# Attention followed by soft-MoE slots on one core: first v cast by the DMA and the second pair's loads issued sooner, warming matmuls ahead of the MoE, last two expert matrices in column halves, output of two batches stored in halves

## The chip, the cores and the metric

The kernel runs on 1 core of one Trainium2 chip. The metric is the device time of one execution in microseconds (us), median of several runs. A profile gives one execution: its span, from the first to the last instruction, is about 1.8 us below the measured time. Engines: PE (matmul), PEld (weight load into PE), DVE, ACT, POOL (whose queue issues the casting DMAs), SP (whose queue issues the stores). To evacuate a tile is to copy it from PSUM, where PE writes, to SBUF. A warming matmul multiplies zeros and its result is thrown away; it is there to keep PE busy, in the hope of keeping its clock up. The granted clock is given as a share: 1.00 is full, 0.50 half. Names in the traces: sc scores, siT slot inputs, hp layer 1, sp layer 2, op output; tpq, tpk and tpv are transposes of q, k and v.

## The reference

```python
# q, k, v: [4 batches, 8 heads, 768, 64] f32; masks: full causal or sink + window, by head
a = softmax(mask(q @ k.T / 8)); x = (a @ v) as [3072 tokens, 512]
logits = x @ phi                              # 3072 x 32 slots
d = softmax(logits, over tokens); slot_input = d.T @ x
for e in range(8):                            # 4 slots each
    h = relu(slot_input[e] @ w1[e])           # 512 -> 1024
    slot_out[e] = h @ w2[e]                   # 1024 -> 512
c = softmax(logits, over slots)
return c @ slot_out                           # 3072 x 512 f32
```

Every output row needs every expert, and the first softmax runs over all tokens. So nothing can be stored before the last attention block and the last weight matrix are in. The inputs are 18.9 MB of q, k, v and 33.6 MB of weights, all f32; the output is 6.29 MB.

## The kernel before

Attention runs over 16 pairs of heads. Beside it the casting queue loads q, k, v of later pairs and the 16 weight matrices (f32 in DRAM, bf16 in SBUF). The parts that matter here:

```python
# start: pair 0 uncast by SP and ACT, cast on DVE and ACT; pairs 1 and 2 by the casting queue
at.load_first("q", nc.sync, stage[0]); at.load_first("k", nc.scalar, stage[1])
at.load_first("v", nc.sync, stage[2])
nc.scalar.dma_start(ri, ...)                  # retrieval flags, 8 KB
at.warm(20)                                   # matmuls on zeros
...
at.load(1); at.load(2)
...
at.transpose(0, "q"); at.transpose(0, "k"); at.warm(3); at.evac(0, "q")
nc.vector.tensor_single_scalar(rne, ri ...)   # waits for the flags
...
at.evac(0, "k"); cast("v", 2, slice(0, 512), nc.vector)
# ... attention ...
# last matrices: 13 whole ones are queued in order, the last in two row halves
# MoE: 4 layer-1 blocks, then layer 2 of 8 experts over two PSUM tiles of 256 columns
for e in range(2, NE): layer2(e)
nc.scalar.activation(slot_out[:, :256], sp[0], ACT.Copy, scale=rcol)
nc.vector.tensor_scalar_mul(slot_out[:, 256:], sp[1], rcol)
# output: matmul, scale on ACT or DVE, store whole rows, 1 to 3 rows of 2 KB per partition
for b in range(B):
    for m in ((1, 2, 3) if b == 0 else (3, 3)):
        ...
        nc.sync.dma_start(ov[:, r:r + m, :], ot[:, :m, :])
```

The softmax here doesn't subtract the row's maximum and nothing guards it: scores larger than these inputs give would overflow.

## Time and profile before

| | kernel before |
|---|---|
| time, median (lowest to highest) | 154.51 us (154.14 to 155.01) |
| span of the profiled run | 152.7 us |
| layer 1 of the MoE starts | 121.49 us |
| last weight bytes move | 132.2 us (only a trickle from 131) |
| first output bytes move | 135.75 us |
| output bytes | 6.29 MB in 15.35 us |

The prediction shows the other views that matter.

```profile
DMA packets 14423, 33.51 MB, mean 219 GB/s; under 512 B 1856, under 2 KB 10496, under 8 KB 12480
q1 hardware_dynamic: 2240, 7.14, 12.5%
```

The second line is SP's queue, the stores and a few first loads: 2240 packets for 7.14 MB, 3.2 KB on average. The casting queue's GB/s count bytes written; it reads twice as many.

### The profile page before, as it was taken

Reading aid. Unit: us, or ns where it says so; the run is one execution under the profiler, and the core shown is the slowest. Engines: PE = TensorE matmul, PEld = TensorE weight load, DVE = VectorE, ACT = ScalarE, POOL = GpSimd, SP = SyncE. Lnnn points to the kernel's source line nnn. Section 1 sums busy time; section 2 is a strip of 40 time slices with the busy share of each in tenths; the row PEclk is TensorE's granted clock in tenths of the full one; section 3 lists DMA queues with packets and bytes.
Section 4 is the critical chain, followed back from the end, with each engine's and each line's share of the span. In section 5 each row is a group of like instructions: output and inputs, shape, how many; then the busy total and the mean of one; then the engine's idle time right before and its main releaser. Section 6 shows DMA issues by size and latency. Waiting matters only on the chain.

```text
span 152.7 us, 5567 instructions
## 1 busy us (share of the span) xinstructions
PE 130.1 (85%) x2397; PEld 86.9 (57%) x2398; DVE 116.2 (76%) x284; ACT 112.5 (74%) x176; POOL 40.2 (26%) x75
## 2 busy tenths in 40 slices
PE   7679998999899999999999999999977799998000
PEld 4436666576577666767767576776636525853000
DVE  6279769989989799898979989888995315189400
ACT  3326779999899899899989889998995224289000
POOL 7624534316243340614425145400000000000000
PEclk9955579999999999999999999999999758999855
DMA  4999999999999999999999999999999999149995
GB/s 135 209 210 203 228 196 227 196 229 197 205 228 194 227 198 225 195 212 222 197 226 198 225 193 215 225 212 212 217 221 210 212 211 181 36 165 416 414 414 240
DMA packets 14423, 33.51 MB, mean 219 GB/s; under 512 B 1856, under 2 KB 10496, under 8 KB 12480
## 3 DMA queue, kind: packets, MB, share of 16 engines
q0 software_dynamic: 11808, 25.63, 88.2%
q1 hardware_dynamic: 2240, 7.14, 12.5%
q10 hardware_dynamic: 352, 0.40, 1.0%
q8 instruction: 18, 0.29, 0.7%
q14 instruction: 5, 0.04, 0.1%
HBM read 52.50 MB, written 6.29 MB: 385 GB/s over the span
## 4 chain that ended last, share of the span: by engine, by line
DVE 42%; PE 32%; ACT 11%; DMA 4%; issue 3%; DVEq 0%; ACTq 0%
DVE xb L162 9%; PE pv L149 7%; ACT pT L123 6%; DVE pT L136 6%; PE sc L114 6%; DVE ot L590 5%; DVE xT L176 5%; DVE pT L133 5%; DMA ri<-in_is_retrieval_dram 4%; DVE vb L103 4%; PE tpx L170 4%; PE hp L516 4%; PE tpv L78 3%; ACT pT L119 3%; PE sp L545 2%
## 5 line engine op out<-in xcount | busy, mean ns | idle before, releaser
L123 ACT ACTIVATE pT<-sc,fb 128x512 bf16<-128x512 f32 (+1 forms) x96 | 52.6, 620 | 4.3 <-PE sc L114 2.8
L119 ACT ACTIVATE pT<-sc 128x1024 bf16<-128x1024 f32 (+1 forms) x48 | 44.8, 952 | 7.3 <-PE sc L114 6.7
L149 PE MATMUL pv<-vb,pT 128*128 128x65 bf16 x672 | 38.0, 197 | 3.6 <-DVE pT L133 2.0
L114 PE MATMUL sc<-qT,kT 64*128 64x256 bf16 (+3 forms) x320 | 36.6, 292 | 0.9 <-DVE kT L91 0.9
L149 PEld LDWEIGHTS <-pT 128*128 128x128 bf16 x672 | 27.1, 99 | 15.4 <-issue 6.9
L136 DVE TENSOR_TENSOR pT<-pT,msk 128x1024 bf16<-128x1024 bf16 (+1 forms) x32 | 19.7, 615 | 0.0
L69 POOL DMA_DIRECT2D qr<-in_q_dram x15 | 9.8, 652 | 34.4 <-PE tpq L78 34.4
L162 DVE TENSOR_TENSOR xb<-pv,rs 128x384 bf16<-128x384 f32 x32 | 17.8, 557 | 1.1
L114 PEld LDWEIGHTS <-kT 64*128 64x128 bf16 x320 | 10.5, 95 | 8.9 <-issue 1.7
L69 POOL DMA_DIRECT2D vr<-in_v_dram x15 | 9.5, 632 | 11.4 <-PE tpv L78 10.7
L176 DVE COPY xT<-tpx 128x768 bf16<-128x768 bf16 (+1 forms) x17 | 9.1, 534 | 4.4 <-PE tpx L170 4.3
L69 POOL DMA_DIRECT2D kr<-in_k_dram x15 | 9.6, 638 | 7.7 <-PE tpk L78 7.6
L133 DVE TENSOR_TENSOR pT<-pT,msk 128x1024 bf16<-128x1024 bf16 x16 | 10.9, 681 | 0.0
L78 PE MATMUL tpq<-ident,qr 96*64 96x96 bf16 x256 | 9.0, 214 | 1.2 <-DVE qr L368 1.2
L170 PE MATMUL tpx<-ident,xb 128*128 128x128 bf16 x96 | 8.2, 220 | 1.9 <-DVE xb L162 1.1
L91 DVE COPY vT<-tpv 128x768 bf16<-128x768 bf16 x16 | 8.7, 547 | 1.4 <-PE tpv L78 1.4
L103 DVE COPY vb<-tpb 128x768 bf16<-128x768 bf16 x16 | 8.9, 557 | 1.1 <-PE tpb L97 1.1
L78 PE MATMUL tpv<-ident,vr 96*64 96x96 bf16 x256 | 9.1, 218 | 0.0
L78 PEld LDWEIGHTS <-vr 96*64 96x64 bf16 x256 | 6.9, 116 | 3.8 <-issue 3.4
L78 PEld LDWEIGHTS <-qr 96*64 96x64 bf16 x256 | 6.7, 113 | 4.1 <-issue 2.5
L78 PE MATMUL tpk<-ident,kr 96*64 96x96 bf16 x256 | 8.8, 214 | 0.0
L91 DVE COPY kT<-tpk 128x768 bf16<-128x768 bf16 x16 | 8.8, 549 | 0.0
(88 smaller groups left out, 156.5 us busy)
## 6 DMA issues: line engine op xcount, KB each, us to landing
w<-in_moe_w_dram POOLq DMA_DIRECT2D x15, 1024.0 KB, 13.3
out_dram<-ot SPq DMA_DIRECT2D x7, 768.0 KB, 6.4
qr<-in_q_dram POOLq DMA_DIRECT2D x15, 192.0 KB, 9.3
kr<-in_k_dram POOLq DMA_DIRECT2D x15, 192.0 KB, 8.9
vr<-in_v_dram POOLq DMA_DIRECT2D x15, 192.0 KB, 8.5
w<-in_moe_w_dram POOLq DMA_DIRECT2D x2, 512.0 KB, 34.2
out_dram<-ot SPq DMA_DIRECT2D x1, 512.0 KB, 2.7
w<-in_k_dram ACTq DMA_DIRECT2D x1, 384.0 KB, 5.3
```

Source lines behind the costliest of these rows:

```text
L69: self.nc.gpsimd.dma_start(t[:96], self.src[w][b, h:h + 2].rearrange("h (p s) d -> p h (s d)", s=8))
L78: self.nc.tensor.transpose(tp[64 * i:64 * (i + 1), s * 96:(s + 1) * 96], src[:96, i, s * 64:(s + 1) * 64], self.ident[:96, :96])
L91: self.nc.vector.tensor_copy(o, i)
L103: self.nc.vector.tensor_copy(self.vbufs[n % 2][:, :, :, :64], tp.rearrange("p (j h d) -> p h j d", j=6, h=2))
L114: nc.tensor.matmul(sc[:, hh, c:c + ni * P], kT[po:po + 64, j * P:(j + 1) * P], qT[po:po + 64, i0 * P:(i0 + ni) * P], start=True, stop=True)
L119: nc.scalar.activation(pT[:, :, :L], sc[:, :, :L], ACT.Exp, scale=self.scale)
L123: nc.scalar.activation(pT[:, hh, :L], sc[:, hh, :L], ACT.Exp, scale=self.scale, bias=fb[:, h + hh:h + hh + 1])
L133: nc.vector.tensor_mul(v, v, m)
L136: nc.vector.tensor_mul(pT[:, :, :L], pT[:, :, :L], self.msk[:, h:h + 2, c:c + L])
L149: self.nc.tensor.matmul(self.pv[n, lo][:, hh, i % 3, :], pT[:, hh, o:o + P], vb[:, hh, j, :65], start=first, stop=True, skip_group_check=True)
L162: nc.vector.tensor_mul(xo, pv[:, :, :, :64], rs.to_broadcast([P, 2, 3, 64]))
L176: self.nc.vector.tensor_copy(self.xT[n // 4][:, n % 4, c], self.tp.pop(("x", n))[:, c])
```

## The change

Its intent is to start the pipeline sooner, to keep PE's clock up near the end, and to fill the hole between the last weight and the first store: with the left 256 columns of the last two w2 matrices loaded first, the left 256 columns of the output of batches 0 and 1 can be computed and stored while the right halves still arrive.

```diff
-        at.load_first("v", nc.sync, stage[2])
-        nc.scalar.dma_start(ri, ...)
+        at.load(0, "v")
+        at.load(1, "qk")
+        nc.sync.dma_start(ri, ...)
 ...
-        at.warm(3)
+        at.warm(4)
         at.evac(0, "q")
+        at.evac(0, "k")
         nc.vector.tensor_single_scalar(rne, ri ...)
 ...
-        at.evac(0, "k")
-        cast("v", 2, slice(0, 512), nc.vector)
 ... (head masks one step later; token logits of known blocks ahead of the last
      transposes; warm(2), warm(4), warm(2), warm(2) in waits before layer 1)
+    w_order = [(i,) for i in range(2 * NE - 2)] + [
+        (i, c, DM // 2) for c in (0, DM // 2) for i in (2 * NE - 2, 2 * NE - 1)]
 ...
-        for e in range(2, NE):
+        for e in range(2, NE - 2):
             layer2(e)
+        at.row_sums(B - 1)
 ... (piece: matmul, scale, store of columns c0 to c0 + cl, staged in the dead w1 tiles)
+        for e in (NE - 2, NE - 1):
+            layer2(e, 0, HALF)
+        slot_cols(0)
+        for b, r, m in ((0, 0, 1), (0, 1, 2), (0, 3, 3), (1, 0, 3), (1, 3, 3)):
+            piece(b, r, m, 0, HALF)
+        for e in (NE - 2, NE - 1):
+            layer2(e, HALF, HALF)
+        slot_cols(1)
+        for b, r, m in ((0, 0, 1), (0, 1, 2), (0, 3, 3), (1, 0, 3), (1, 3, 3)):
+            piece(b, r, m, HALF, HALF)
+        for b in range(2, B):
+            for r in (0, 3):
+                piece(b, r, 3)
```

## The prediction

> **What bounds the kernel now.** I read the forty slices first, then stretches cut where the DMA row changes, then the chain of waits at both ends. The slices show what the total hides:
>
> ```profile
> PEclk9955579999999999999999999999999758999855
> DMA  4999999999999999999999999999999999149995
> ```
>
> The first line is the granted TensorE clock, the second the busy share of the 16 DMA engines. DMA is busy almost everywhere except for one hole (the 1 and the 4), and the clock is low twice: early, and just ahead of the hole. By stretches (start:end, length, busy of PE, PEld, DVE, ACT, POOL, then clock, DMA share, GB/s):
>
> ```profile
> 2.00:6.00 4.00, 2.94 (x17) 1.95 (x15) 1.99 (x11) 1.04 (x1) 3.78 (x6) 1.00 0.96 267
> 6.00:7.00 1.00, 0.89 (x26) 0.69 (x28) 0.73 (x3) 0.77 (x2) 0.00 (x0) 1.00 0.54 111
> 20.00:60.00 40.00, 38.08 (x782) 26.05 (x782) 37.25 (x91) 37.28 (x58) 13.81 (x23) 0.98 1.12 211
> 98.00:128.50 30.50, 27.09 (x483) 16.91 (x486) 20.80 (x51) 21.41 (x38) 0.35 (x1) 0.89 1.03 214
> 128.50:132.50 4.00, 4.00 (x123) 3.35 (x116) 1.18 (x2) 0.94 (x2) 0.00 (x0) 1.00 0.37 74
> 132.50:135.75 3.25, 2.83 (x50) 2.07 (x44) 1.82 (x4) 1.91 (x4) 0.00 (x0) 1.00 0.00 0
> 135.75:151.10 15.35, 5.00 (x18) 2.00 (x16) 7.12 (x12) 5.51 (x10) 0.00 (x0) 0.77 1.01 410
> 151.10:152.70 1.60, 0.00 (x0) 0.00 (x0) 0.00 (x0) 0.00 (x0) 0.00 (x0) 0.50 0.00 0
> ```
>
> Three regimes. To about 120 us attention is bound by compute: in 20 to 60 us PE, DVE and ACT are each over 93% busy, and no wait for an attention input appears after the first pair. Beside it the weights stream at 211 to 214 GB/s written; the casting queue reads twice what it writes, so this is some 420 GB/s read, the same rate as the stores' 410. From 128.5 the stream runs dry, and until 135.75 the DMA engines do 4.00 x 0.37 = 1.5 us of work in 7.25 us: a hole of 5.8 us. Then the 6.29 MB of output take 15.35 us, and 1.6 us pass from the last byte to the end. So everything after 135.75 is fixed by bytes, and the time is set by when the first store can start, which the chain of waits puts on PE:
>
> ```profile
> 1.25 6.83 DMA ri<-in_is_retrieval_dram
> 8.10 0.38 DVE rne L380
> 8.93 0.47 DVE kT L91
> 9.45 0.61 PE sc L114 x4
> ...
> 121.49 1.90 PE hp L516 x14
> 123.39 0.44 PE tpe L205 x3
> 123.83 1.83 PE hp L516 x16
> ...
> 128.18 0.98 PE hp L516 x16
> ...
> 130.72 2.54 PE sp L545 x88
> 133.29 0.48 ACT slot_out L567
> ```
>
> Above: DVE waits for the 8 KB retrieval flags until 8.10, and only then evacuates kT, so the first scores wait to 9.45. Below: the MoE chain from siT to slot_out is PE without a gap, and four equal layer-1 blocks take 1.9, 1.83, 1.45 and 0.98 us: the clock is half in the first ones. No DMA stands in that chain, so the weights are in time.
>
> **What the Trainium skill says.** "TensorE: Matmul & The Clock Gate", Part 1: a free-running window of 3413 ns decides between half and full clock by PE's activity; Part 4: transposes don't count as busy in the same way. The trace agrees: cut at multiples of 3.41 us, the clock reads 0.98 in 4.27:7.69, 0.50 in 7.69:11.10, 1.00 from 21.30, 0.99 in 116.90:120.30, 0.50 in 120.30:123.70, 0.51 to 127.10 and 1.00 after it. The window that loses the clock at 120.3 had PE busy 2.22 of 3.40 us, part of it transposes. "DMA: Bandwidth & Descriptors", Issuing engines are not separate DMA queues: all queues share the same 16 engines, and issuing from several only saves issue time. The trace agrees (a share about 1 with one queue or three), so starting v and pair 1 on the casting queue gives no bandwidth. Same page, Why small descriptors are slow: about 3 cycles fixed per packet; I use it for an estimate below.
>
> **The change part by part.**
> 1. *Start.* v of pair 0 is cast by the DMA: its DVE cast (0.68 us) goes. The casting queue issues first at about 1.2 us instead of 1.84, so its data arrive some 0.6 us earlier. kT is evacuated before the flags: the second transpose group ends at 7.29, so kT can run 7.3 to 7.85 instead of 8.84, and scores begin near 8.0, 1.4 us earlier. I take off 0.2 us because q and k now meet the casting queue's traffic earlier. The masks still need the flags at about 8.1, but two of them take 0.5 us each and mask(0,0) then falls near 10.8 instead of 12.05, so the shift carries through. PE is full from 14.5 to 21.3, so it reaches attention's end: **-1.2 us**. Perhaps one clock window earlier at full speed too (up to -0.5, not counted).
> 2. *Between attention and MoE.* Token logits of known blocks move ahead of the last transposes, and 2+4+2+2 warming matmuls of 128x256 fill waits that are there (0.86 before the first, 0.23, 0.34 and 0.38 us). At full clock one is about 0.11 us (20 took 3.81, most of them cold). Their own cost is about 0. If they keep the clock, layer 1 becomes 4 x 1.0 instead of 1.90+1.83+1.45+0.98 = 6.16: -2.1; two transposed blocks 0.25 instead of 0.44: -0.4. Together **-2.5 us**. I give this 65%.
> 3. *Column halves.* The left columns need only half of the last two matrices: 2.1 MB read later, at 420 GB/s 5 us, are not waited for. On PE the two experts cost 32 matmuls for 512 columns, at 2.54/88 = 29 ns each 0.9 us, of which half, 0.45, leaves the path; six row-sum matmuls (0.4) come onto it. Sum **0**. The order of waits shows that left matmuls wait for the left loads only, and left stores for left evacuations only.
> 4. *Stores.* Before, slot_out at 133.29 led to the first data at 135.75: 2.5 us (0.48 + 0.5 matmul + 0.5 evacuation + 1.0 issue). The chain stays. First data then: 135.75 - 1.2 - 2.5 = **132.05**.
> 5. *Is it continuous from there?* The left part is 12 x 128 x 256 x 4 bytes = 1.57 MB, 3.8 us, to 135.9. Its 12 evacuations (475 to 485 ns, two engines) need about 2.9 us and keep ahead. The right half needs its loads: the old stream ended by 132.5; I take 0.4 off for the earlier start and add 0.6 for 512-byte packets (twice to sixteen times as many as now: an estimate from the skill's 3 cycles over 32 to 64 of payload), so about 132.7. Then PE 0.45, slot_out 0.48, matmul 0.2, evacuation 0.48, issue 0.9 makes 135.2, before the left stores end. So hardly a gap; I allow 0.2, and 0.2 for stores of 1 KB runs.
>
> Sum: 132.05 + 15.35 + 0.4 + 1.6 = 149.4 us of span, against 152.7: -3.3. Weighing part 1's possible extra gives -3.5. The measured time is 1.8 us above the span (154.51 against 152.7).
>
> **Rivals.**
> - *The clock stays low* in 120 to 127 us (35%): the window's phase is not ours, and warm matmuls may be too few. Then first data at 134.5, span about 151.9: time near 153.5. For it: PE's idle time there is real and transposes are many. Against: every gap on the path is filled.
> - *The right half becomes the wait.* If 512-byte packets ran a quarter slower, the last 4.2 MB would take 2.5 us longer, with the left stores taking a share of the same engines: right columns near 137.5, a gap of about 2 us, time near 152.8. For it: these are the smallest large packets of the kernel. Against: q, k and v already go in 1 KB packets, and 20 to 60 us, with them, moves 211 GB/s against 214 for the stretch with weights nearly alone.
> - *The start gives nothing*, because masks, the flags or PE at half clock decide: +1.2, time near 152.2. Against: PE's own order waits only for kT.
> - *The bytes bind*: 58.8 MB at 420 GB/s are 140 us, plus 2 at the start and 1.6 at the end: span 143.6 is a floor, far enough away.
>
> **Range and chances.** With the clock kept I get 150.3 to 151.7, without 152.5 to 153.8; the mixture has its middle at 151.1. The 2% line is 151.42, so the better branch is mostly across it and the other is not. Range 149.7 to 153.4; faster 0.58, same 0.40, slower 0.02. Nothing here adds more than a microsecond of work to a bound engine, so slower is remote.
>
> **What would show it.** Scores begin at about 8.0 us and attention ends 1.2 us earlier (1); clock 1.0 through layer 1, blocks of 1.0 us each (2); first store data near 132 (4), DMA hole under 3 us in all and no second hole between the halves (5); 15.4 us of store data in all. It is wrong if layer 1 runs at half clock, if a DMA wait stands before the right half's layer 2, or if the total of DMA time grows by over 1 us through the smaller packets.

## The result, and the profile after

| | before | changed |
|---|---|---|
| median (lowest to highest) | 154.40 us (154.14 to 155.01, 4 runs) | 152.51 us (151.94 to 152.79, 4 runs) |
| span of the profiled run | 152.7 us | 151.1 us |
| ratio | | 0.9867 (95% interval 0.9826 to 0.9908) |

The changed kernel is 1.3% faster, which is within 2%. A ratio is the mean time of one kernel's fast runs over that of the other's fast runs of the same rounds, so it isn't quite the ratio of the medians.

First the forty slices of the changed kernel: clock, DMA share and GB/s.

```profile
PEclk9999999999999999999999999999999999999955
DMA  3899999999999999999999999999999999999995
GB/s 121 163 210 205 225 197 228 195 221 204 203 226 198 223 203 225 197 206 225 200 225 199 220 201 208 220 221 215 213 215 215 204 194 198 127 321 343 386 413 210
```

The hole is gone from the DMA row and the second clock dip from the clock row. But the last slices no longer read 416 414 414: they climb from 321 over 343 and 386 to 413. The stretches say when (same columns as in the prediction; the first line is the start, which moves 200 GB/s instead of 267):

```profile
2.00:6.00 4.00, 3.59 (x19) 2.24 (x17) 2.15 (x10) 0.70 (x2) 3.92 (x8) 1.00 0.72 200
...
125.00:128.50 3.50, 3.50 (x64) 1.76 (x56) 1.18 (x2) 0.99 (x2) 0.00 (x0) 1.00 1.46 198
132.40:137.00 4.60, 3.59 (x32) 2.17 (x32) 3.25 (x8) 3.67 (x10) 0.00 (x0) 1.00 1.01 332
137.00:141.50 4.50, 3.53 (x12) 1.38 (x11) 4.36 (x8) 4.00 (x7) 0.00 (x0) 1.00 1.03 343
141.50:149.20 7.70, 0.00 (x0) 0.00 (x0) 0.20 (x1) 0.00 (x0) 0.00 (x0) 0.64 1.02 416
149.40:151.10 1.70, 0.00 (x0) 0.00 (x0) 0.00 (x0) 0.00 (x0) 0.00 (x0) 0.50 0.00 0
```

From 132.4 to 141.5, as long as half rows go out, the DMA engines are fully busy and move only 332 to 343 GB/s; from 141.5, with whole rows, 416. All the output takes 132.2 to about 149.3, 17.1 us, against 15.35 before. The first store data came 3.5 us earlier (132.2 against 135.75), and 1.7 us of that went back into slower stores. The engines' share of 1.46 at 198 GB/s in 125 to 128.5 is where the half matrices are read: b_start, an experiment below that loads whole matrices, has a share of 1.05 and 213 GB/s in the same stretch.

The chain of waits, end of it, in order of time (start, length, what):

```profile
102.98 30.53 DMA w<-in_moe_w_dram
133.56 0.43 PE sp L548 x8
134.00 0.48 ACT slot_out L574
```

Before, PE alone stood here. Now the load of the last right half does, and PE waits for it, though in this profile only by about 0.15 us (the eight matmuls before it began at 133.01 and took 0.40). The timeline shows the start and layer 1:

```profile
8.44 0.61 PE L114 MATMUL sc<-qT,kT 64*128 64x256 bf16 x4
...
120.53 1.05 PE L520 MATMUL hp<-w,siT 128*32 128x512 bf16 x16 [0.15 <-DVE siT L510]
```

Scores start at 8.44 instead of 9.45, layer 1 at 120.53 instead of 121.49, and its first block runs at full clock. A warning goes with the first of these lines: four score matmuls take 0.61 us here as in the kernel before, where the clock record read 0.50; at full clock four take 0.39. So PE ran at half speed up to about 20 us in this run too, and the record's 9s in the first slices are wrong. The packets:

```profile
DMA packets 20663, 33.31 MB, mean 220 GB/s; under 512 B 1952, under 2 KB 17952, under 8 KB 18848
q1 hardware_dynamic: 4688, 6.76, 12.8%
```

There are 7456 more packets under 2 KB. The average packet of SP's queue fell from 3.2 to 1.4 KB.

### The profile page after: what moved, and what is told of

Its sections match the earlier page's. It is cut to its first block, busy times and chain, and to the rows that moved or that the text cites. A ratio compares the mean times of both kernels' runs of the same rounds, so it can differ in the third digit from the quotient of the medians.

```text
span 151.1 us, 5539 instructions
## 1 busy us (share of the span) xinstructions
PE 132.0 (87%) x2372; PEld 87.9 (58%) x2372; DVE 116.0 (77%) x287; ACT 114.4 (76%) x183; POOL 43.0 (28%) x77
## 4 chain that ended last, share of the span: by engine, by line
DMA 32%; DVE 24%; PE 21%; ACT 8%; issue 6%; POOL 2%; DVEq 0%; POOLq 0%; ACTq 0%
DMA w<-in_moe_w_dram 20%; DMA vr<-in_v_dram 8%; DVE xb L162 6%; PE pv L149 5%; PE sc L114 5%; DVE pT L136 4%; ACT pT L123 4%; DVE pT L133 3%; DMA w<-in_q_dram 3%; PE tpv L78 3%; DVE vb L103 3%; DVE xT L176 3%; PE tpx L170 2%; POOL w L275 2%; ACT pT L119 2%
## 5 line engine op out<-in xcount | busy, mean ns | idle before, releaser
L69 POOL DMA_DIRECT2D vr<-in_v_dram x16 | 10.4, 649 | 9.5 <-PE tpv L78 9.3
L594 DVE TENSOR_SCALAR w<-op,rrow 128x256 f32<-128x256 f32 (+1 forms) x18 | 9.2, 568 | 2.8 <-PE op L589 2.7
L589 PE MATMUL op<-slot_out,expT 128*128 128x256 bf16 (+1 forms) x36 | 7.9, 306 | 2.0 <-ACT slot_out L574 1.1
L275 POOL DMA_DIRECT2D w<-in_moe_w_dram x10 | 6.8, 680 | 8.9 <-DMA w<-in_moe_w_dram 7.0
L592 ACT ACTIVATE w<-op,rrow 128x256 f32<-128x256 f32 (+1 forms) x18 | 8.7, 543 | 0.8 <-PE op L589 0.7
```

What stands on the lines that cost most here:

```text
L69: self.nc.gpsimd.dma_start(t[:96], self.src[w][b, h:h + 2].rearrange("h (p s) d -> p h (s d)", s=8))
```

## The experiments

Each kernel was run in 5 rounds beside the kernel before. The first eight ran on one chip, the last four on another; across the two, ratios to the kernel before are compared, not times. All were correct. All runs were fast, except one of the kernel before beside the first eight: its median (154.33) counts it, the ratios leave it out.

**The changed kernel again** (after_again).

> The changed kernel once more, as the yardstick of this round: about 152.5 us, 1.2% under the kernel before. In its profile the first store data should come near 132, 3.5 us before the kernel before has them, and the stores of half rows should again move only about 340 GB/s where whole rows move 410.

Measured: 152.19 us, ratio 0.9849 (0.9817 to 0.9882). But its profile differs from the first one: layer 1 starts at 118.56, and the first store data come at about 130.6. The time hardly followed (span 150.5 against 151.1). PE's timeline near the end shows where the 1.6 us went: "0.21 <-DMA" in brackets is the idle time before and what ended it.

```profile
128.07 0.40 PE L548 MATMUL sp<-w,hT 128*32 128x256 bf16 x8 [0.21 <-DMA w<-in_moe_w_dram]
...
133.35 0.62 PE L548 MATMUL sp<-w,hT 128*32 128x256 bf16 x8 [1.51 <-DMA w<-in_moe_w_dram]
```

The right half lands at the same time, however early PE is. The left stores then run out first and a hole reopens: DMA share 0.68 in 135 to 137.

**Half rows in the kernel before** (b_split).

```diff
-                nc.sync.dma_start(ov[:, r:r + m, :], ot[:, :m, :])
+                for c0 in ((0, 256) if b < 2 else (0,)):
+                    cl = 256 if b < 2 else DM
+                    nc.sync.dma_start(ov[:, r:r + m, c0:c0 + cl], ot[:, :m, c0:c0 + cl])
```

> The kernel before, with one edit: the stores of the first two batches are issued as a left and a right column half (runs of 1 KB instead of whole rows of 2 KB and more), both late, nothing else moved. Theory A (half rows are slow in themselves, 340 instead of 410 GB/s for 3.15 MB): 9.25 - 7.7 = 1.6 us slower than the kernel before. Theory B (the stores of the changed kernel were slow because the last weights were still being read beside them): no reads here, so within 0.3 us of the kernel before.

Measured: 156.05 us against 154.33, ratio 1.0098: 1.7 us slower by the medians. SP's queue, and two stretches of its stores, first half rows, then whole ones:

```profile
q1 hardware_dynamic: 4752, 7.14, 13.7%
137.00:143.00 6.00, 3.51 (x13) 1.38 (x11) 5.63 (x9) 4.02 (x7) 0.00 (x0) 1.00 1.00 339
144.50:152.00 7.50, 0.00 (x0) 0.00 (x0) 0.00 (x0) 0.00 (x0) 0.00 (x0) 0.50 1.03 417
```

339 GB/s with nothing being read beside it, and 416 in the kernel before in the same 137 to 143 us: theory A holds and theory B falls.

**Half rows only on the SBUF side** (b_sbuf).

```diff
-                ot = osb.tile([P, 3, DM], F32, tag="ot", name="ot")
+                ot = osb.tile([P, 6, 320], F32, tag="ot", name="ot")   # 256 used, 64 of padding
 ...
-                nc.sync.dma_start(ov[:, r:r + m, :], ot[:, :m, :])
+                nc.sync.dma_start(ov6[:, 2 * r:2 * (r + m), :], ot[:, :2 * m, :256])   # b < 2
```

> The kernel before, with the tiles of the first two batches padded in SBUF so that each half row of 1 KB lies apart there, while one store writes whole contiguous rows in DRAM, in order. If 1 KB pieces are the cost (theory A1), about 1.6 us slower, as with the column halves. If it is the skipping between half rows on the DRAM side (theory A2), within 0.3 us of the kernel before.

Measured: 155.79 us, ratio 1.0101, the same loss.

```profile
q1 hardware_dynamic: 4672, 7.14, 13.6%
137.00:143.00 6.00, 3.59 (x13) 1.38 (x11) 5.71 (x9) 4.11 (x8) 0.00 (x0) 1.00 1.01 337
```

DRAM is written in whole contiguous rows here, and still 337 GB/s. So it is the size of the pieces, not the skipping in DRAM. The packets agree: the queue has 4672 instead of 2240, and these 2432 more are just what comes of cutting 5 x 128 contiguous runs into 12 x 2 x 128 half rows. A piece breaks where either side breaks. The whole rows are stored mostly three at a time, in runs of 6 KB; where between 1 and 6 KB the rate falls was not tried.

**No early store** (a_fullstore).

```diff
-            nc.sync.dma_start(ov[:, r:r + m, c0:c0 + cl], ot[:, o:o + m, c0:c0 + cl])
+            if c0 + cl == DM:
+                nc.sync.dma_start(ov[:, r:r + m, :], ot[:, o:o + m, :])
```

> The changed kernel without the early store: left columns are still computed early, but batches 0 and 1 are stored as whole rows after their right columns. First store data then near 136 as in the kernel before (right loads land at 133.5, then 0.45 + 0.5 + 0.2 + 0.5 + 0.9), and 15.35 us of stores at 410 GB/s. If the early store gains the 3.8 us of hole and loses 1.6 by half rows, this is about 2 us slower than the changed kernel, so about equal to the kernel before. If the early store is worth nothing, equal to the changed kernel.

Measured: 154.92 us, ratio 1.0028; 2.7 us slower than the changed kernel of the same round, so about equal to the kernel before (interval 0.9999 to 1.0057).

```profile
133.00:136.40 3.40, 2.38 (x18) 1.34 (x16) 1.10 (x3) 1.79 (x4) 0.00 (x0) 0.50 0.00 0
136.60:151.40 14.80, 5.52 (x16) 1.97 (x15) 5.75 (x10) 5.13 (x9) 0.00 (x0) 0.62 1.02 414
```

The hole is back, whole rows move at 414, and the balance is as expected: the early store fills it and pays part of it back.

**No column halves** (a_nohalf): w2 loads, layer 2 and slot_out as in the kernel before, all output in whole rows.

```diff
-    w_order = [(i,) for i in range(2 * NE - 2)] + [
-        (i, c, DM // 2) for c in (0, DM // 2) for i in (2 * NE - 2, 2 * NE - 1)]
+    w_order = [(i,) for i in range(2 * NE - 1)] + [(2 * NE - 1, 2)]
 ... (layer2 over sp[0] and sp[1]; slot_out by ACT and DVE; piece(b, r, m) for all)
```

> The changed kernel without the column halves: weights, layer 2 and slot_out as in the kernel before, output in whole rows, new start and new tail order kept. PE is then done early and the last weight is the wait: it lands about 132.5, slot_out about 133.5, first store data about 135, 15.35 us of stores, so a span of 152 and a time about 1 us above the changed kernel. If the halves are worth what they were meant for (the whole hole), about 3 us above it; if they only move bytes about, equal.

Measured: 156.68 us (155.73 to 157.84), ratio 1.0156: 4.5 us slower than the changed kernel and 2.4 slower than the kernel before. Both expectations of the size were too low. PE waits for each of the last three loads, its clock falls to half, and the output matmuls then run at half speed: in the first 3.3 us of stores the DMA engines move 362 GB/s. In this profile about 1 us of the loss is something else: at its end, from 151.8 to 152.8 us, a last bit of the output moves at a DMA share of 0.08 (the same is seen in b_warm25 below).

```profile
132.00:136.20 4.20, 2.99 (x18) 1.12 (x18) 1.44 (x3) 1.80 (x3) 0.00 (x0) 0.50 0.00 0
136.20:139.50 3.30, 3.30 (x10) 1.20 (x9) 2.90 (x5) 2.64 (x5) 0.00 (x0) 0.52 0.93 362
```

**No warming matmuls at the end** (a_nowarm).

```diff
-        at.warm(2)                # and warm(4), warm(2), warm(2)
         at.token_logits(b, 0, range(3, 4))
```

> The changed kernel without the ten warming matmuls near the end. If they are what keeps the clock, it falls to half near 120, layer 1 takes 1.9 us a block again, slot_out comes up to 2.5 us later and the time is up to 2 us above the changed kernel. If the earlier arrival or the new order of the token logits keeps it, no difference.

Measured: 152.25 us against 152.19. Layer 1 does lose its clock:

```profile
116.63 1.90 PE L515 MATMUL hp<-w,siT 128*32 128x512 bf16 x16 [0.38 <-DVE siT L506]
118.90 1.90 PE L515 MATMUL hp<-w,siT 128*32 128x512 bf16 x16
...
133.70 0.40 PE L543 MATMUL sp<-w,hT 128*32 128x256 bf16 x8 [1.54 <-DMA w<-in_moe_w_dram]
```

Yet it starts at 116.63, so early that two slow blocks still leave PE 1.54 us ahead of the last weight. The warming matmuls hold the clock (this run shows it in one profile) and are worth nothing in these runs. Whether they pay in a run whose attention ends late, as in the first profile of the changed kernel, wasn't isolated.

**The new start alone** (b_start): the kernel before with the start's part of the diff.

> The kernel before with the new start alone (v and pair 1 on the casting queue, flags later, masks one place later). Attention should end 0.9 to 1.2 us earlier; the first store follows the end of the MoE chain on PE, so 0.9 us faster if the weights are still in time, 0 if the last weight becomes the wait at once.

Measured: 155.07 us, ratio 1.0034 (0.9997 to 1.0072): not faster, perhaps slower. PE's timeline:

```profile
127.80 0.62 PE L544 MATMUL sp<-w,hT 128*32 128x256 bf16 x16 [1.05 <-DMA w<-in_moe_w_dram]
130.29 0.29 PE L544 MATMUL sp<-w,hT 128*32 128x256 bf16 x4 [1.88 <-DMA w<-in_moe_w_dram]
132.70 0.83 PE L544 MATMUL sp<-w,hT 128*32 128x256 bf16 x12 [2.12 <-DMA w<-in_moe_w_dram]
```

Layer 1 starts at 116.67, 4.8 us earlier than before. The three waits for weights add up to 1.05 + 1.88 + 2.12 = 5.05 us. The last weights come when they came before (last bytes at 132.1 us against 132.2), so the gain is swallowed whole, and PE, now cold, does the first output matmuls at a clock of 0.50.

**The old start in the changed kernel** (a_oldstart): the start's part of the diff undone.

> The changed kernel with the old start. If the start is worth something here it is about 0.9 us slower than the changed kernel; if the right half's loads set the end, it is equal.

Measured: 153.70 us, ratio 0.9949; 1.5 us slower than the changed kernel. Layer 1 starts at 121.08, first store data come at 132.8, and PE doesn't wait for the right half. So the start pays where a left half can use it.

**Why the start moves attention by so much.** The first scores tell PE's early clock better than the clock record does. Time of the first four score matmuls, and when layer 1 starts, in all profiles:

| start | kernels (first four scores in us; layer 1 starts) |
|---|---|
| old | before (0.61; 121.49), b_split (0.61; 121.45), b_sbuf (0.61; 121.33), a_oldstart (0.61; 121.08) |
| new | changed (0.61; 120.53), changed again (0.61; 118.56), a_oneearly (0.61; 117.63), a_warmright (0.39; 116.90), a_fullstore (0.39; 116.80), b_start (0.39; 116.67), a_nowarm (0.39; 116.63), a_nohalf (0.39; 116.55) |
| old, 25 warming | b_warm25 (0.39; 120.84), a_oldstart_warm25 (0.39; 121.02) |

With the new start PE is at full clock from the first scores, or a few microseconds later, in seven of eight profiles, and layer 1 then starts 3 to 5 us earlier than with the old start. The early clock's own part is smaller, 2 to 4 us: the eighth profile, at half clock until about 20 us, has 120.53. Each kernel has one profile, so how often the clock comes up early in its other runs isn't known. Two runs try whether PE's idle time ahead of the first transposes is the reason.

**Five more warming matmuls at the old start** (b_warm25: at.warm(25) instead of at.warm(20) in the kernel before).

> The kernel before with 25 warming matmuls at the start instead of 20, nothing else. In four profiles with the old start the first scores ran at half speed (0.61 us for four) until 18 to 21 us; in five of six with the new start they ran at full speed from 8 to 11 us. Theory C (PE's idle time of 1.2 us before the first transposes is what loses the early clock): the first four scores take 0.39 us, attention ends 3 to 4 us earlier, and yet the time stays within 0.7 us of the kernel before, because PE then waits for the last weights. Theory D (the loads or the flags make the difference): scores stay at 0.61 us until about 20 and nothing moves.

Measured: 155.84 us, ratio 1.0079 (1.0045 to 1.0113). Neither theory came out. The first scores took 0.39 us, but by 11.8 us 16 transposes took 0.85 again where the full clock gives 0.53, and layer 1 started at 120.84. In this run the first store data came at 135.0, earlier than before, yet the span is longer: from 150.5 to 152 a last bit of the output dribbles at a DMA share of 0.07, about one engine of 16.

```profile
135.00:150.00 15.00, 4.99 (x18) 1.99 (x16) 7.12 (x12) 5.50 (x10) 0.00 (x0) 0.83 1.01 409
150.50:152.00 1.50, 0.00 (x0) 0.00 (x0) 0.00 (x0) 0.00 (x0) 0.00 (x0) 0.50 0.07 29
```

What makes the last bytes late there was not found, nor whether it is so in the other runs of this kernel. Of the other profiles only a_nohalf's has it.

**The same in the changed kernel with the old start** (a_oldstart_warm25).

> The changed kernel with the old start and 25 warming matmuls. If the start's 1.4 us in the changed kernel are the early clock, this regains them: about 152.2 us, the same as the changed kernel. If they are the place of the loads and the flags, it stays at about 153.7.

Measured: 153.06 us, 152.02 to 154.10, ratio 0.9898 (0.9853 to 0.9942), between a_oldstart's 0.9949 and the changed kernel's 0.9849, with overlapping intervals. Inconclusive; in its profile the early clock was again lost by 11.7 us. So in these two profiles warming alone doesn't hold it. Which part of the new start does (kT no longer waiting for the flags, which leaves PE 1.2 us idle just there, or v in bf16) stays open.

**Ten warming matmuls before the right half** (a_warmright).

```diff
+        at.warm(10)
         for e in (NE - 2, NE - 1):
             layer2(e, HALF, HALF)
```

> The changed kernel with ten warming matmuls between the left output matmuls and the right half of layer 2, where PE waits 1.5 us for the last weight and its clock falls. If the half clock after that wait counts, the first right store comes some 0.3 us earlier and the time falls by that; if the stores' bytes set the end there, no difference.

Measured: 153.20 us (151.64 to 153.75), ratio 0.9888 (0.9842 to 0.9934), not told apart from the changed kernel. The profile shows the idea backfiring:

```profile
132.34 2.34 PE L62 MATMUL waste<-zeros 128*128 128x256 bf16 x10
134.61 1.04 PE L548 MATMUL sp<-w,hT 128*32 128x256 bf16 x16
```

The clock had fallen earlier, in the wait for the left half, so the ten took 2.34 us instead of the 1.1 I had counted, and the right half began at 134.61, 0.8 to 1.3 us later than in the profiles in which PE stood waiting for its last load (133.35 to 133.84).

**Only one batch early** (a_oneearly): the list of early pieces cut to batch 0.

> The changed kernel with only batch 0 stored early in halves, batches 1 to 3 in whole rows. Half rows fall from 3.15 to 1.57 MB, which saves 0.8 us of store time, but the left stores then last only 2.3 us, from about 130.6 to 133, and the DMA engines wait for the right half's first store near 136.2: a hole of some 3 us instead of 0.65. Expected 1 to 1.5 us slower than the changed kernel. If half rows were the main loss and the hole not, 0.8 us faster.

Measured: 153.75 us, ratio 0.9946 (0.9914 to 0.9978) against 0.9849 of the changed kernel: about 1% slower, 1.5 us. The hole opens where it was expected:

```profile
134.00:137.00 3.00, 2.43 (x16) 1.24 (x9) 1.31 (x3) 1.85 (x4) 0.00 (x0) 0.50 0.15 51
```

Fewer small pieces don't pay for an idle DMA stretch, so two batches are near the right amount. No run beat the changed kernel.

## Why the prediction was right or wrong

The time, 152.51 us, lies in the range, 1.4 us above the middle; "faster by over 2%", held likelier, did not come true. That it lies in the range is luck. The clock was kept, and for that case the prediction gave 150.3 to 151.7; 152.51 is inside only because the range also covered the case of the low clock, which didn't happen. (Nor is 151.1 the middle of the mixture: 65% of about 151.0 and 35% of about 153.15 is 151.7.) Of the prediction's own three signs of being wrong two came: a DMA wait before the right half's layer 2 (some 0.15 us in the first profile, 1.51 in the second), and over 1 us more of DMA time.

- **What bounds it** held: the moment of the first store, and then bytes. "First data then: ... 132.05" measured 132.2, though in part because errors cancel: the start gave 0.24 us too little and layer 2 cost 0.25 more, but slot_out to first data took 2.1 instead of 2.5. In the second profile of the changed kernel the first store no longer sets the time: it comes 1.6 us sooner still, for 0.6 us of span, because the last loads stand behind it.
- **Step 1, the start.** "Scores begin near 8.0" measured 8.44 with PE at half clock; in the five profiles at full clock it was 7.7 to 8.1. Attention's end, read from layer 1's start, came 0.96 us earlier instead of 1.2 in that profile, and a_oldstart's 121.08 says that some 0.4 of it is the new order of the tail. The term left out, "perhaps one clock window earlier (up to -0.5, not counted)", was mis-sized: in seven of eight profiles with the new start the clock was up earlier, and layer 1 began 2.9 to 4.9 us earlier than before. That did not move the end in proportion, because the last loads stand behind it. b_start shows it: 4.8 us earlier, 5.05 us of waits. The rival that "the start gives nothing" was right for the kernel before and wrong for the changed one, where undoing it costs 1.5 us.
- **Step 2, the clock**, came true as to the clock (1.05 us a block), and as to the -2.5 us it was right for the profiled run, whose attention ended late (on PE's timeline layer 2 begins 7.49 us after layer 1 before, 5.00 after). It was not needed in the runs that ended early: without the warming matmuls the time is the same. What the cited Part 4 says of transposes no run here tests by itself.
- **Step 3, the halves.** PE's sum of 0 came to +0.25: from the first layer-2 matmul to slot_out it took 4.31 us before (128.98 to 133.29) and 4.56 after (125.53 to 130.09). And "left matmuls wait for the left loads only" hid a wait: PE stood 0.21 us for the left loads in the changed kernel's second profile, and 1.66 to 2.58 in three that were earlier still (a_oneearly, a_warmright, a_fullstore).
- **Step 5 is the step that failed**, in the term "and 0.2 for stores of 1 KB runs". It measured 17.1 us of stores instead of 15.35, so 1.7 us: 3.15 MB at 339 instead of 417 GB/s is 9.3 instead of 7.6 us. b_split and b_sbuf show it by themselves. I had put nearly all of the cost of small packets on the loads, where the estimate was good: 2.1 MB written at 198 instead of the 213 GB/s of whole matrices (b_start in the same stretch) is 0.75 us against the 0.6 allowed. Still the right half landed at 133.35 to 133.84, not 132.7: the term "0.4 off for the earlier start" gave nothing. In b_start, with the new start and whole matrices, PE got the last weight at 132.70, not at 132.1; with the 0.75 that makes 133.45.
- **The rival of the right half** named the right wait and nearly the right time (152.8), but in the first profile for the wrong reason: no idle stretch opened between the halves, only slower stores.

The sum, redone for the profiled run: predicted span 149.4; first data +0.15, stores +1.3 (17.05 against 15.75), from the last byte to the end +0.25 (1.85 against 1.6): 151.1.

## What to carry to other kernels

A transfer that is cut up so that part of it can start early can pay for the cut in its rate: here 1 KB pieces lost 17 to 19%. Work out the rate from the smallest contiguous piece on either side before counting the gain, and cut only as much as fills the idle stretch. When a compute chain and a stream of loads end nearly together, shortening the chain alone may yield nothing, as in b_start, until the stream's consumer is split as well.

## What the Trainium skill lacked or had wrong

- "DMA: Bandwidth & Descriptors", Specifications, gives 512 B as the smallest transfer for line rate, and Why small descriptors are slow about 3 cycles a packet. Stores of 1 KB pieces ran at 337 to 343 GB/s where whole rows, most of them in runs of 6 KB, ran at 414 to 417, a loss of 17 to 19%. Those 3 cycles, on 32 for 1 KB at the page's 32 bytes a cycle, are by estimate at most 9%. No table there has stores by piece size for this chip. "Perfetto Trace Analysis", DMA Optimizations, with its "Small DMAs (< 2KB) have significant per-transfer overhead", fits better if it is read for pieces (the transfers themselves were of 128 KB and more), and I had not used it.
- No page gives the cost of a gap that is on the SBUF side alone. It splits the pieces just as a gap in DRAM does: 4672 against 4752 packets, and 337 against 339 GB/s, in b_sbuf and b_split.
- "TensorE: Matmul & The Clock Gate", Part 1, warns that clock records can be unreliable. The runs show one form of it: the record reads 1.00 in 7 to 20 us while four score matmuls take 0.61 us, as they do at 0.50, instead of 0.39.
- The same Part calls the warm-up penalty under 1% of a span. Here, with the same new start, layer 1 began at 120.53 with half clock until about 20 us and at 116.55 to 118.56 with full clock sooner: 2 to 4 us of 151. The time followed by less: the changed kernel's two profiles, at 120.53 and 118.56, have spans of 151.1 and 150.5 us.
